# A decode layer on one core: the last 1,664 bytes a row of the modulation's weights loaded as 126 rows and 2 rows instead of 128

## Chip, cores, metric

One core of one Trainium2 chip. The metric is device time in microseconds (us) of one execution. Executions have a fast and a slow state (of the kernel before mostly 436.1 to 437.0 us, and 444.4 to 444.6). A ratio is the mean time of one kernel's fast runs over that of the other's fast runs of the same rounds, so it is not quite the ratio of the medians that are quoted.

## The reference, cut to what matters

```
mod = (silu(c) @ w_mod)                       # w_mod: 1024 x 6144, split into six shifts, scales and gates
h   = layernorm(x) * (1 + ca) + sa
x   = x + ga * attention(h, k_cache, v_cache, wq, wo)     # batch 8, 32 heads on 4 KV heads, 8192 keys of 128
h   = layernorm(x) * (1 + cb) + sb
x   = x + gb * ((relu(h @ W_gate) * (h @ W_up)) @ W_down) # 1024 -> 3584 -> 1024
```

All of it is bf16, one token for each of eight batches. The inputs are 185.6 MB, read once. That is what takes the time: 98.9% of sixteen DMA engines' span, by the page below.

## The kernel before

All weights and caches come through one ring in SBUF (`arena`, 128 partitions). SyncE issues the loads in a fixed order, each as soon as the part of the ring that it overwrites has been read.

```
def load(key, src, n, lo):
    place[key] = lo
    stream.append((key, src, n, lo))

def pump():
    while stream:
        key, src, n, lo = stream[0]
        if P.unread("arena", lo, lo + n):
            return
        stream.pop(0)
        dst = arena[:, lo:lo + n]
        P.op("sp", lambda e, dst=dst, src=src: e.dma_start(dst, src), writes=[slot_r(lo, lo + n)], dma=True, ...)
...
load(("wm", 0), wm_src[:, 0:D], D, 0)                    # D = 1024: the modulation's weights, 2,048 bytes a row,
load(("wm0", 0), wm_src[:, D:24 * D], 23 * D, D)         # 47,104 bytes a row,
load(("wm", 1), wm_src[:, 24 * D:48 * D], 24 * D, 24 * D) # 49,152 bytes a row
# [cut: wq in two loads; for each batch two K loads and a V load; wo, gate, up]
wd_parts = [(0, 14), (14, 21), (21, 25), (25, 27), (27, 28)]
for i, (r0, r1) in enumerate(wd_parts):
    load(("wd", i), d_src[:, r0 * D:r1 * D], (r1 - r0) * D, VPART + r0 * D)
```

The second half of the modulation's matmuls reads `slot_r(place["wm", 1], ... + 24 * D)`, so it waits for whatever loads fill that stretch.

Of the kernel before, what the change touches and what calls it, by code (L numbers as in the profile page):

```python
# [263 lines left out]
def bass_adaLN_cond__gqa_block_cached__glu_gated_reglu__decode_kernel(nc, A_x, A_k_cache, A_v_cache, A_wq, A_wo, B_x, B_W_gate, B_W_up, B_W_down, c, w_mod, out):  # L264
    B, _, D = A_x.shape
# [15 lines left out]
    KF = F // 128  # L281
    KO = Hq * Dh // 128
    FJ = F // 4

    P = Prog()
    holding = []
# [6 lines left out]
    with ExitStack() as es:  # L293
        E = es.enter_context

        def sb(name, shape, dtype):
            return E(nc.sbuf_tensor(name, shape, dtype))
# [4 lines left out]
        arena = sb("arena", [128, RING], dt.bfloat16)  # L302
# [38 lines left out]
        oX = ktb[:, 1024:2048].rearrange("p (k b) -> p k b", b=32)  # L341
        hrow = ktb[:, 2048:2048 + FJ]
        hmT = sb("hmT", [128, KF, 33], dt.bfloat16)
        xg = sb("xg", [64, 2, 256], dt.float32)
        rsel2 = sb("rsel2", [128, 64], dt.float32)
        grel = ktb[:, 4096:4096 + 2 * FJ].bitcast(dt.float32)
        r_oX, r_hmT = ("kt", 1024, 2048), ("hmT", 0, 1)
# [22 lines left out]
        def bank(b, n=1):  # L370
            return ("ps", b, b + n)

        def slot_r(lo, hi):
            return ("arena", lo, hi)
# [2 lines left out]

        stream, place = [], {}

        def load(key, src, n, lo):  # L380
            place[key] = lo
            stream.append((key, src, n, lo))

        def pump():
            while stream:
                key, src, n, lo = stream[0]
                if P.unread("arena", lo, lo + n):
                    return
                stream.pop(0)
                dst = arena[:, lo:lo + n]  # L390
                P.op("sp", lambda e, dst=dst, src=src: e.dma_start(dst, src), writes=[slot_r(lo, lo + n)], dma=True,  # L391
                     own=key[0] if key[0] in ("ka", "kb", "v") else None)
                if key[0] in ("ka", "kb", "v"):
                    P.held[key] = (lo, lo + n)

        wm_src = w_mod.rearrange("(p k) n -> p (k n)", k=KC)
# [3 lines left out]
        u_src = B_W_up.rearrange("(p k) n -> p (k n)", k=KC)  # L400
        d_src = B_W_down.rearrange("(p k) n -> p (k n)", k=KF)
        load(("wm", 0), wm_src[:, 0:D], D, 0)
        load(("wm0", 0), wm_src[:, D:24 * D], 23 * D, D)
        load(("wm", 1), wm_src[:, 24 * D:48 * D], 24 * D, 24 * D)
        wq_parts = [(0, 4), (4, 8)]
        for i, (r0, r1) in enumerate(wq_parts):
            load(("wq", i), wq_src[:, r0 * 4096:r1 * 4096], (r1 - r0) * 4096, 48 * D if i == 0 else 0)
# [11 lines left out]
        head = stream[2:]  # L419
        del stream[2:]  # L420
        pump()
        for t, src in enumerate((c.rearrange("b (j n) -> (b j) n", j=4), A_x.rearrange("b o (j n) -> (b o j) n", j=4))):
            P.op("act", lambda e, t=t, src=src: e.dma_start(cx[:, t, :], src), writes=[R("cx", t, t + 1)], dma=True)
        stream.extend(head)
        P.pump = pump
        pump()


# [102 lines left out]
        for i, (r0, r1) in enumerate(wq_parts):  # L531
            lo, hi = place["wq", i], place["wq", i] + (r1 - r0) * 4096
# [11 lines left out]
        for z in range(2):  # L544
            src = ps[:, 4 + z, :].rearrange("p (u x r) -> p u r x", u=J, r=2)
            dst = qs[:, 16 * z:16 * z + 16, :].rearrange("p (u r) x -> p u r x", r=2)
# [146 lines left out]
        for z in range(2):  # L693
# [6 lines left out]
            dst = orow[:, 4 * z:4 * z + 4, :].rearrange("p j d -> p (j d)")  # L700
# [34 lines left out]

        H = FJ // 2
        for nm, b0 in (("gate", 0), ("up", 2)):
            lo, hi = place[nm, 0], place[nm, 0] + KC * F
# [9 lines left out]
        for h in range(2):  # L748
            P.op("act", lambda e, h=h: e.activation(grel[:, H * h:H * h + H], ps[:, h, 0:H], ACT.Relu), reads=[bank(h)],
                 writes=[("kt", 4096 + FJ * h, 4096 + FJ * h + FJ)])  # L750
            P.op("dve", lambda e, h=h: e.tensor_tensor(out=hrow[:, H * h:H * h + H], in0=ps[:, 2 + h, 0:H],  # L751
                                                       in1=grel[:, H * h:H * h + H], op=ALU.mult),
                 reads=[bank(2 + h), ("kt", 4096 + FJ * h, 4096 + FJ * h + FJ)], writes=[("kt", 2048 + H * h, 2048 + H * h + H)])
        P.op("dve", lambda e: e.transpose(hmT[:, :, 1:33], hrow.rearrange("p (x k) -> p k x", k=KF)),  # L754
             reads=[("kt", 2048, 2048 + FJ), r_hmT], writes=[r_hmT])
        for i, (r0, r1) in enumerate(wd_parts):
            lo, hi = place["wd", i], place["wd", i] + (r1 - r0) * D
# [51 lines left out]
```

## Time and profile before

| kernel before | |
|---|---|
| median of the first three runs | 436.33 us (436.11 to 444.56) |
| profiled run | 444.49 us, slow state |
| bytes of the loads, share of sixteen DMA engines' span | 185.61 MB, 98.9% |
| end of the last load to end of the program | 3.0 us |

How to read it: the page counts sixteen DMA engines. A load of 128 rows leaves 128 packets in the trace, one a row, and sixteen landings, one an engine, so an engine has eight rows of such a load. The trace keeps the time of every landing. Sorted, they show how far apart the engines are, though not which is which. The lines of the profile are shown with the prediction, just below.

### The profile page before, as it was taken

What the parts mean: (1) busy time and instruction counts of PE and PEld (TensorE: products, weight loads), DVE (VectorE), ACT (ScalarE), POOL (GpSimd) and SP (SyncE); (2) the same over time, 40 slices, a digit from 0 to 9 for tenths busy, and PEclk for the clock granted to TensorE, in tenths of its full rate; (3) what the DMA queues carried; (4) which work ended last, traced back from release to release, by engine and by line L of the source; (5) the groups of instructions that cost most, each with busy time, mean ns of one, the idle gap of its engine ahead of it and who ended that gap; (6) DMA issues with size and microseconds to landing.
All of it is one profiled execution on the core that took longest, in us unless ns stands there. A gap on an engine that the chain in (4) does not pass through costs nothing. (4 is left out here: it accounts for less than half of the span.)

```text
span 443.1 us, 4774 instructions
## 1 busy us (share of the span) xinstructions
PE 263.3 (59%) x2139; PEld 138.0 (31%) x1979; DVE 249.0 (56%) x342; ACT 29.5 (7%) x54; POOL 8.7 (2%) x22
## 2 busy tenths in 40 slices
PE   0324336728865783886578388658838865365157
PEld 0100002218225421822542172154217215241015
DVE  0603028872985697298569729756972975421020
ACT  1100010020001002000100200010020010100000
POOL 3000000000000000000000000000000000000000
PEclk9976657978996997799599889959968996865668
DMA  9999999999999999999999999999999999999995
GB/s 367 417 355 390 404 385 426 379 417 430 467 396 420 456 444 420 429 470 390 435 476 408 423 429 467 420 423 473 399 420 426 467 455 402 452 416 419 439 414 239
DMA packets 5494, 185.74 MB, mean 419 GB/s; under 512 B 656, under 2 KB 752, under 8 KB 1136
## 3 DMA queue, kind: packets, MB, share of 16 engines
q1 hardware_dynamic: 5360, 185.61, 98.9%
q8 instruction: 5, 0.08, 0.1%
q10 hardware_dynamic: 128, 0.04, 0.0%
q14 instruction: 1, 0.01, 0.0%
HBM read 185.63 MB, written 0.02 MB: 419 GB/s over the span
## 5 line engine op out<-in xcount | busy, mean ns | idle before, releaser
L576 DVE STREAM_TRANSPOSE kt<-arena 128x1024 uint32<-128x1024 uint32 x128 | 148.2, 1211 | 64.4 <-DVEq L181 47.3
L586 PE MATMUL ps<-kt,qpad 128*128 128x512 bf16 x512 | 133.9, 384 | 44.1 <-DVE kt L576 38.1
L626 PE MATMUL ps<-arena,pT 128*64 128x256 bf16 x1024 | 74.5, 320 | 51.8 <-PEq L181 51.8
L626 PEld LDWEIGHTS ps<-arena,pT 128*64 128x64 bf16 x1024 | 72.0, 132 | 53.7 <-issue 53.1
L586 PEld LDWEIGHTS ps<-kt,qpad 128*128 128x128 bf16 x512 | 40.5, 98 | 133.7 <-DVE kt L576 101.0
L616 DVE TENSOR_SCALAR pT<-pd,mqf 128x1024 bf16<-128x1024 bf16 x64 | 28.2, 503 | 0.6
L608 ACT ACTIVATE prb<-ps,bias 128x1024 bf16<-128x1024 f32 x16 | 17.7, 1109 | 139.8 <-DVE mjt L603 139.8
L614 DVE STREAM_TRANSPOSE pd<-prb 128x1024 bf16<-128x1024 bf16 x16 | 19.8, 1239 | 10.9 <-ACT prb L608 10.9
L592 DVE TENSOR_REDUCE negm<-ps 128x1 f32<-128x512 f32 x32 | 21.2, 661 | 4.5 <-PE ps L586 4.5
L744 PE MATMUL ps<-arena,hT 128*32 128x448 bf16 x128 | 11.1, 535 | 16.8 <-DMA arena<-in_B_W_up_dram 11.4
L751 DVE TENSOR_TENSOR kt<-ps,kt 128x448 bf16<-128x448 f32 x2 | 1.2, 618 | 27.6 <-PE ps L744 27.6
L514 PE MATMUL ps<-arena,hT 128*32 128x512 bf16 x96 | 10.3, 615 | 9.7 <-DMA arena<-in_w_mod_dram 9.7
L538 PE MATMUL ps<-arena,hT 128*32 128x512 bf16 x64 | 7.2, 631 | 14.6 <-DMA arena<-in_A_wq_dram 14.6
L645 ACT ACTIVATE oacc<-ps 128x32 f32 (+1 forms) x9 | 1.8, 197 | 159.4 <-PE ps L640 159.4
L521 DVE COPY mod<-ps 128x512 f32<-128x512 f32 x2 | 1.3, 670 | 19.3 <-PE ps L514 19.3
L567 POOL TENSOR_TENSOR qpad<-qR,mq 128x128 bf16<-128x128 bf16 x8 | 4.9, 608 | 319.2 <-DVE pT L616 260.8
L549 DVE CAST kt<-ps 128x512 bf16<-128x512 f32 x1 | 0.7, 691 | 18.2 <-PE ps L538 18.2
L744 PEld LDWEIGHTS ps<-arena,hT 128*32 128x32 bf16 x64 | 2.4, 140 | 25.7 <-DMA arena<-in_B_W_up_dram 12.0
L763 PE MATMUL ps<-arena,hmT 128*32 128x256 bf16 x112 | 8.3, 309 | 3.5 <-DVE hmT L754 3.1
L714 PE MATMUL ps<-arena,kt 128*32 128x256 bf16 x128 | 5.9, 373 | 5.1 <-DMA arena<-in_A_wo_dram 5.1
L598 PE MATMUL ps<-identf,negm 128*128 128x128 f32 x16 | 3.9, 326 | 7.8 <-DVE negm L596 7.8
L763 PEld LDWEIGHTS ps<-arena,hmT 128*32 128x32 bf16 x112 | 6.5, 109 | 5.6 <-DMA arena<-in_B_W_down_dram 4.9
(87 smaller groups left out, 80.9 us busy)
## 6 DMA issues: line engine op xcount, KB each, us to landing
arena<-in_A_k_cache_dram SPq DMA_DIRECT2D x16, 4096.0 KB, 27.5
arena<-in_A_wq_dram SPq DMA_DIRECT2D x2, 4096.0 KB, 38.3
arena<-in_B_W_gate_dram SPq DMA_DIRECT2D x1, 7168.0 KB, 24.7
arena<-in_B_W_up_dram SPq DMA_DIRECT2D x1, 7168.0 KB, 27.9
arena<-in_w_mod_dram SPq DMA_DIRECT2D x1, 6144.0 KB, 33.4
arena<-in_w_mod_dram SPq DMA_DIRECT2D x1, 5888.0 KB, 17.8
arena<-in_B_W_down_dram SPq DMA_DIRECT2D x1, 3584.0 KB, 19.7
arena<-in_B_W_down_dram SPq DMA_DIRECT2D x1, 1792.0 KB, 23.6
```

Source lines behind the costliest of these rows:

```text
L514: fns.append(lambda e, w=w, pr=pr, j=j, kk=kk: hold(e.matmul(ps[32 * j:32 * j + 32, pr, :], hT[:, kk, :], w[:, 2 * pr:2 * pr + 2, j, :], s ...
L538: fns.append(lambda e, w=w, r=kk - r0, z=z, g=g, kk=kk: hold(e.matmul(ps[32 * g:32 * g + 32, 4 + z, :], hT[:, kk, :], w[:, r, g, z, :], st ...
L576: P.op("dve", lambda e_: e_.transpose(ktb[:, to:to + PART].bitcast(dt.uint32), arena[:, lo:lo + PART].bitcast(dt.uint32)), reads=[slot_r(l ...
L586: fns.append(lambda e_, t=t, r=r: e_.matmul(ps[:, e // 4, :].rearrange("p (c k) -> p c k", k=32), qpad[:, t * 2 + r, 24 - 8 * i:152 - 8 * ...
L592: P.op("dve", lambda e: e.tensor_reduce(negm[:, h:h + 1], ps[:, h, :], AX.X, ALU.max, negate=True), reads=[bank(h)] + (free(("ka", b)) if ...
L608: P.op("act", lambda e: e.activation(prb[:, f, :], ps[:, 2 * f:2 * f + 2, :].rearrange("p h n -> p (h n)"), ACT.Exp, bias=bias[:, 0:1], sc ...
L614: P.op("dve", lambda e: e.transpose(pd[:, f], prb[:, f]), reads=[R("prb", f, f + 1)], writes=[R("pd", 1024 * f, 1024 * f + 1024)])
L616: P.op("dve", lambda e, g=g: e.tensor_scalar(out=pT[:, f, :, :, g, :], in0=pd[:, f].rearrange("p (c i x) -> p c i x", c=32, i=2), scalar1= ...
L626: fns.append(lambda e, n=n, h=h, c_=c_, i=i, t=t: e.matmul(ps[64 * t:64 * t + 64, 5, 0:2 * Dh].rearrange("p (i d) -> p i d", d=Dh), pT[:, ...
L714: fns.append(lambda e, w=w, k=k, j=j: e.matmul(ps[32 * j:32 * j + 32, 5, 0:256], oX[:, k, :], w[:, k, j, :], start=(k == 0), stop=(k == KO ...
L744: fns.append(lambda e, w=w, kk=kk, h=h, j=j, b0=b0: hold(e.matmul(ps[32 * j:32 * j + 32, b0 + h, 0:H], hT[:, kk, :], w[:, kk, j, h, :], st ...
L763: fns.append(lambda e, w=w, r=k - r0, k=k, i2=i2, j=j: e.matmul(ps[32 * j:32 * j + 32, 4, 0:256], hmT[:, k, 1 - i2:33 - i2], w[:, r, i2, j ...
```

## The change

Two of the sixteen DMA engines are to carry 13 KB less, on the thought (an inference of the author's, not shown) that they are the ones that come last. The last 832 elements (1,664 bytes) a row of the modulation's weights are taken out of their load and brought by one of 126 rows and one of 2.

```
+    UNEVEN = [(832, 126)]
...
-        def load(key, src, n, lo):
+        def load(key, src, n, lo, dst=None):
             place[key] = lo
-            stream.append((key, src, n, lo))
+            stream.append((key, src, n, lo, arena[:, lo:lo + n] if dst is None else dst))
...
-        load(("wm", 1), wm_src[:, 24 * D:48 * D], 24 * D, 24 * D)
+        at1 = 48 * D - sum(n for n, rows in UNEVEN)
+        load(("wm", 1), wm_src[:, 24 * D:at1], at1 - 24 * D, 24 * D)
+        for n, rows in UNEVEN:
+            for lo, part in ((0, slice(0, rows)), (n // 2, slice(rows, 128))):
+                load(("wm1", n, lo), wm_src[part, at1:at1 + n], n // 2, at1 + lo, arena[part, at1:at1 + n])
+            at1 += n
```

More of the change, by code (lines that the diff above doesn't have):

```diff
@@ L378, in bass_adaLN_cond__gqa_block_cached__glu_gated_reglu__decode_kernel @@
         stream, place = [], {}
-        def load(key, src, n, lo):
+        def load(key, src, n, lo, dst=None):
             place[key] = lo
-            stream.append((key, src, n, lo))
+            stream.append((key, src, n, lo, arena[:, lo:lo + n] if dst is None else dst))
         def pump():
             while stream:
-                key, src, n, lo = stream[0]
+                key, src, n, lo, dst = stream[0]
                 if P.unread("arena", lo, lo + n):
@@ L389, in pump @@
                 stream.pop(0)
-                dst = arena[:, lo:lo + n]
                 P.op("sp", lambda e, dst=dst, src=src: e.dma_start(dst, src), writes=[slot_r(lo, lo + n)], dma=True,
```

## The prediction

It came to this: -0.49 us on the two spared engines, +0.14 us on the others (nine packets of 70 ns, 0.63 us, less 0.49), and +0.21 us on two of these that get a tenth packet. That 126 rows go to fourteen engines was assumed. That the two spared are the two last of the end (440.10 and 440.12) was the author's inference; "then they land at 440.11 - 0.49" starts from it, and the 0 in "-0.06 to 0 us" is the case in which the next laggard is one with a tenth packet (440.13). The forecast is 436.2 - 0.1 = 436.1 us.

> **What bounds the kernel now.** I read the page first: its row of DMA slices and its table of queues.
>
> ```profile
> DMA  9999999999999999999999999999999999999995
> ...
> q1 hardware_dynamic: 5360, 185.61, 98.9%
> q8 instruction: 5, 0.08, 0.1%
> ...
> q14 instruction: 1, 0.01, 0.0%
> ```
>
> The sixteen DMA engines are busy in every slice but the last. The loads (q1) take 98.9% of sixteen engines' span, for 185.61 MB. Two small queues fetch instructions on the same engines. No compute engine comes near: the page has PE at 59% and DVE at 56%. So the kernel streams its inputs once, and its time is the streaming time plus a head and a tail. Next, the sums by stretch (columns: stretch, length, busy time of PE, PEld, DVE, ACT, POOL, then granted clock, DMA share, GB/s):
>
> ```profile
> 5.00:45.00 40.00, 11.95 (x101) 2.29 (x37) 10.61 (x26) 2.50 (x4) 0.40 (x2) 0.84 1.00 389
> ...
> 120.00:160.00 40.00, 27.18 (x202) 14.54 (x202) 29.17 (x38) 2.50 (x5) 0.63 (x1) 0.91 1.00 433
> ```
>
> Both stretches have a DMA share of 1.00, but the first moves 389 GB/s and the other 433. The profiled run is one of the slow state (444.49 us). Its packets tell what that is: one of 32,768 bytes takes 1,353 to 1,361 ns for most of the first 80 us and 1,213 ns from there on. At the later rate those 80 us would have been about 80 x (1359 - 1213) / 1359 = 8.6 us shorter, and 444.5 - 8.6 = 435.9 is close to the two fast runs, 436.11 and 436.33. So I compare with 436.2, and read the tail of this profile as that of a fast run too.
>
> Then the chain of waits, its last pieces (start, duration, what):
>
> ```profile
> 413.18 26.30 DMA arena<-in_B_W_down_dram
> 439.49 0.04 issue
> 439.53 0.61 PE ps L763 x8
> 440.14 0.02 issue
> 440.16 0.41 PE ps L763 x4
> 440.58 0.02 issue
> 440.60 0.43 DVE lu L767
> 441.03 0.02 issue
> 441.05 0.42 DVE ob L769
> ```
>
> The end hangs on the last loads of W_down: eight matmuls, then four more, for the last two row groups, two vector instructions, the store. The last four matmuls start at 440.16, when the final load has landed on its slowest engine. Everything after that is fixed, 3.0 us to the span's end.
>
> Last, the issues in the timeline of SyncE:
>
> ```profile
> 0.00 1.44 SPq L391 DMA_DIRECT2D arena<-in_w_mod_dram  x3
> 1.57 23.59 SPq L391 DMA_DIRECT2D arena<-in_A_wq_dram  x2
> ...
> 343.66 0.33 SPq L391 DMA_DIRECT2D arena<-in_A_v_cache_dram  x1
> 361.64 0.33 SPq L391 DMA_DIRECT2D arena<-in_A_wo_dram  x1
> ```
>
> The load ahead of the V load issued at 343.66 is done on its first engine only at 348.66. That is the pattern of all batches: a load is issued at least some 5 us before any engine is through with the one ahead. So no engine runs dry, and a lag that one engine has picked up is neither lost nor made good: it is carried to the end.
>
> The trace keeps the sixteen completion increments of each load, one an engine, though not which engine gave which. The last load's are at 438.18 to 438.62 (ten engines), 439.10, and then 439.78, 439.82, 439.92, 440.10, 440.12. The program ends on the very last. Followed back, load by load, the six laggards left the pack one at a time, each after an instruction-fetch packet: 16,384 bytes at 50.17, 104.19, 393.79, 410.50 and 436.56 us (879 to 1,119 ns each), and 8,192 bytes at 84.72. A 16 KB fetch costs its engine about 1.2 to 1.6 us of lag, and each of the five fell on another engine.
>
> [...]
>
> **The change part by part.** Rates from the fast part of this trace: 32,768 bytes in 1,213 ns and 2,048 bytes in 84 ns, hence about 27.2 bytes a ns and 8 to 9 ns a packet. A packet of 1,664 bytes should take 61 + 9 = 70 ns (an estimate from those two).
> - Removed: the big load's rows shrink from 49,152 to 47,488 bytes. Each engine has eight of them, so 8 x 1,664 = 13,312 bytes less, 13,312 / 27.2 = 0.49 us on each of the sixteen.
> - Added: [...] Two more issues on SyncE, at 0.33 to 0.43 us each. They move the first wq issue from 1.57 to about 2.4 us, while the weights of the modulation land at 34.49: hidden by 30 us.
> - [...] Total bytes are unchanged, so the pack does not gain; only the two relieved engines move.
> - The matmuls on the second half of the weights must now wait for three loads instead of one. They start up to 0.2 us later at 34.5, with over 15 us of loads queued behind: not on the path that sets the end.
>
> What this does to the end depends on who is last. The engines of the two last increments at the end (440.10 and 440.12) come, followed back, from the late edge of the pack. One was hit by the first fetch: the first wq load's increments reappear in the second 10.75 us later, all but the one next to last, 45.25, which reappears at 57.64. The other was hit at 393.79, out of the pack's last two (387.79 and 387.81). [...] Then they land at 440.11 - 0.49 = 439.62, and the next laggard, 439.92, which got nine small packets, becomes the last: 439.92 + 0.14 = 440.06[...]. Against 440.12: -0.06 to 0 us. I choose -0.1 us, leaning a little to the gain because neighbouring small packets overlap: the last load has 8 x 2,048 bytes an engine and adds 0.62 to 0.65 us to the increments, where 8 x 84 would be 0.67.
>
> **Rivals.**
> - The two relieved engines alone set the end in unprofiled runs (the other fetches cost less there). For it: a fetch's cost differs with the traffic, 879 to 1,119 ns. Against it: three other engines are within 0.35 us of the last. It would give -0.49 us: 435.7.
> - The relieved engines are not among the laggards. For it: increments carry no engine. Then the last one gets its nine small packets for nothing, +0.14 to +0.21 us: 436.4.
> - The 126-row load is split over the engines in a way that makes them write across each other, or falls on far fewer engines. With one engine, it would take 126 x 70 = 8.8 us there, carried to the end: 445, slower by just 2%. The first would add some tenths. Nothing in this profile tells of it[...].
> - A wait replaces a wait: the two extra loads delay the modulation. Hidden, as worked out: no change.
>
> **Range and chances.** The centre is 436.2 - 0.1 = 436.1 us. The named outcomes lie between 435.7 and 436.4, and the two fast runs of before differ by 0.2 us; I add 0.3 to 0.5 us for runs on another chip: 435.4 to 436.9. A shift of 2% is 8.7 us, eighteen times the largest gain that 13 KB can give an engine, so "faster" gets 0.005. "Slower" gets 0.01, for the single-engine split or medians caught by the slow state; "within 2%" gets 0.985.
>
> **What would show it.** Right: the 126-row load's semaphore is at 2 at once and climbs by fourteen landings; among the last load's sixteen increments, two of the five latest move forward by about 0.6 us against the pack; the pack itself lands 0.1 to 0.2 us later; SyncE's first issues are five for the modulation; loads of wq, K and V keep their spacing (9.65 us for 4 MB). Wrong: increments of the last load in the old pattern[...], a pack later by more than 0.3 us (small rows dearer than 70 ns, or colliding), or a DMA share under 0.95 in a stretch that had 1.00 (an engine ran dry, and lags are not simply carried). A fast time under 435.4 would mean that the lags are worth more than this trace shows.

## The result

| | median us | range | runs |
|---|---|---|---|
| before | 436.7 | 436.11 to 444.56 | 6 |
| changed | 436.5 | 436.41 to 438.13 | 6 |

The ratio of the fast runs is 1.0003, 95% interval [0.9988, 1.0019]: the same. A second set on another chip (five runs against nine, told below) gave 1.001 [0.9996, 1.0024]. Nothing here is clear of noise in time. What the change did has to be read from the traces.

The changed kernel's profile is of the fast state. These lines answer to those in the prediction: first its DMA row, the same two queues, and two stretches of the sums by stretch (same columns).

```profile
DMA  9999999999999999999999999999999999999996
...
q1 hardware_dynamic: 5504, 185.61, 98.9%
q8 instruction: 5, 0.08, 0.1%
```

```profile
5.00:45.00 40.00, 13.97 (x133) 2.90 (x53) 10.60 (x26) 2.50 (x4) 0.40 (x2) 0.81 1.00 427
120.00:160.00 40.00, 28.37 (x203) 15.64 (x204) 29.02 (x38) 2.50 (x5) 0.63 (x1) 0.87 1.02 441
```

The loads move the same bytes in 144 more packets: 128 of 1,664 bytes and sixteen of 4 bytes, one for each new landing. The trace shows how the two small loads were shared out. The semaphore of the 126-row load has one update at 2.08 us, at its issue, and then fourteen landings, 31.53 to 32.26; that of the 2-row load one at 2.48 us and two landings, 31.99 and 32.08. That is nine rows and one, if they are shared out evenly. In the first stretch they move 427 GB/s where the slow profile of before had 389: that is the state, not the change. The kernel before in its fast state, run again as an experiment below, has 428 there, and its 32,768-byte packets take 1,213 ns from the start. (This view counts the whole of a packet in the stretch in which it starts. A share of 1.02 with 441 GB/s is thus no more than full, and in a short stretch one row of sixteen 32,768-byte packets, 0.52 MB, more or less moves the figure a good deal.)

Then SyncE's first issues in the timeline, and the end of the chain of waits, of the changed kernel:

```profile
0.00 2.31 SPq L391 DMA_DIRECT2D arena<-in_w_mod_dram  x5
2.35 22.06 SPq L391 DMA_DIRECT2D arena<-in_A_wq_dram  x2
```

```profile
403.30 20.43 DMA arena<-in_B_W_down_dram
423.73 0.04 issue
423.77 8.92 PE ps L768 x112
432.69 0.02 issue
432.71 0.43 DVE lu L772
433.14 0.02 issue
433.17 0.42 DVE ob L774
```

Five issues for the modulation instead of three, and the first wq issue at 2.35 us, as foreseen. The chain's end looks different from the slow profile: 112 matmuls in one piece after the first W_down load, with no wait for the last one. In fact two paths tie. The last load lands on its slowest engine at 432.23 us; its four matmuls (0.04 + 0.41 us, by the slow profile's chain) would end at 432.68, and the 112 end at 432.69. Both paths begin at the landing of the slowest engine, so the lag of the engines counts on either.

For a comparison within one state, the kernel before was run again (first experiment). Its chain ends like this:

```profile
402.91 20.35 DMA arena<-in_B_W_down_dram
423.26 0.04 issue
423.30 8.99 PE ps L763 x112
```

The landing that starts the matmuls is 0.47 us earlier there than in the changed kernel (423.26 against 423.73).

### The profile page after: what moved, and what is told of

Read it like the earlier page. It is cut to its first block, busy times and chain, and to the rows that moved or that the text cites. A ratio compares the mean times of both kernels' runs of the same rounds, so it can differ in the third digit from the quotient of the medians.

```text
span 435.2 us, 4777 instructions
## 1 busy us (share of the span) xinstructions
PE 260.5 (60%) x2139; PEld 137.9 (32%) x1979; DVE 249.1 (57%) x342; ACT 29.5 (7%) x54; POOL 8.8 (2%) x22
## 5 line engine op out<-in xcount | busy, mean ns | idle before, releaser
L749 PE MATMUL ps<-arena,hT 128*32 128x448 bf16 x128 | 9.8, 481 | 19.3 <-DMA arena<-in_B_W_up_dram 12.1
L543 PE MATMUL ps<-arena,hT 128*32 128x512 bf16 x64 | 7.2, 631 | 11.8 <-DMA arena<-in_A_wq_dram 11.8
L519 PE MATMUL ps<-arena,hT 128*32 128x512 bf16 x96 | 9.1, 559 | 8.3 <-DMA arena<-in_w_mod_dram 8.3
```

What stands on the lines that cost most here:

```text
L519: fns.append(lambda e, w=w, pr=pr, j=j, kk=kk: hold(e.matmul(ps[32 * j:32 * j + 32, pr, :], hT[:, kk, :], w[:, 2 * pr:2 * pr + 2, j, :], s ...
L543: fns.append(lambda e, w=w, r=kk - r0, z=z, g=g, kk=kk: hold(e.matmul(ps[32 * g:32 * g + 32, 4 + z, :], hT[:, kk, :], w[:, r, g, z, :], st ...
L749: fns.append(lambda e, w=w, kk=kk, h=h, j=j, b0=b0: hold(e.matmul(ps[32 * j:32 * j + 32, b0 + h, 0:H], hT[:, kk, :], w[:, kk, j, h, :], st ...
```

## The experiments

The landings and packet durations in this table are read from the traces. Head is the median landing of the second load, which no edit touches; all else is counted from it or from the last load, so that a slow start of a run (two have it, head at 17.9 us) drops out. The pack is the median of the ten earliest of the last load's sixteen landings.

| kernel | first wq packet on its 16 engines, ns, min / median / max | pack minus head, us | last landing minus pack, us | ratio to before [95%] |
|---|---|---|---|---|
| before, again | 1213 / 1213 / 1213 | 413.46 | 1.57 | 1.0005 [0.9988, 1.0022] |
| changed | 1471 / 1604 / 1616 | 414.02 | 1.44 | 1.0003 [0.9988, 1.0019] |
| changed, again | 1346 / 1552 / 1665 | 414.08 | 1.58 | 1.0010 [0.9996, 1.0024] |
| even split | 1213 / 1213 / 1214 | 413.58 | 2.07 | 1.0002 [0.9985, 1.0019] |
| 112 + 16 rows | 1325 / 1424 / 1440 | 413.68 | 1.92 | 1.0013 [0.9996, 1.0030] |
| even split, four times as wide | 1213 / 1213 / 1213 | 413.52 | 1.98 | see its text |
| 112 + 16, four times as wide | 1354 / 1882 / 2098 | 415.09 | 2.06 | 1.0032 [1.0016, 1.0049] |
| 126 + 2, four times as wide | 1359 / 1883 / 2367 | 415.33 | 1.71 | 1.0038 [1.0021, 1.0055] |

The theory that the prediction left me with (relief): the unequal load spares two engines half a microsecond (13,312 bytes at 27.2 bytes a ns), the rest pay only for their small packets. Its rival, raised when the changed kernel's trace showed the first wq packets at 1,471 to 1,616 ns: the packets of an uneven split and those of the loads beside it slow each other down (collision). The author thought it was because the rows change engines there; no trace has the engine of a row, so this cannot be shown. What the runs test is the slowing. In the changed kernel's trace the 1,664-byte packets start 66 ns apart on an engine, until engines that are already on wq appear; then packets take 75 to 118 ns instead of 69.

**The kernel before, again.** No edit.

> The kernel before, unchanged, for a profile in the fast state and for the noise of a ratio. All theories: ratio 1.000 within 0.002. In its profile the first packet of 32,768 bytes of the wq load takes 1,213 ns on each engine (in the changed kernel's profile it took 1,471 to 1,616 ns). The last load's sixteen landings have a pack of ten or so and six later ones, as in the slow profile; the two very last are 0.15 to 0.2 us behind the third last.

Measured: 436.42 us median (436.17 to 437.21), profile fast, first wq packets at 1,213 ns on all sixteen engines. The last load landed at 430.03 to 430.40 (ten engines), 431.09, 431.55, 431.71, 431.78, 431.78 and 431.80: a pack and six laggards. The three last are within 0.02 us, not 0.15 to 0.2 us apart from the third, so that detail of the slow profile was chance. Sparing two of the six can move the last landing by 0.02 us at most.

**Even split.** The same bytes in a load of their own, all 128 rows:

```
-            for lo, part in ((0, slice(0, rows)), (n // 2, slice(rows, 128))):
-                load(("wm1", n, lo), wm_src[part, at1:at1 + n], ...)
+            load(("wm1", n, rows), wm_src[:, at1:at1 + n], n, at1)
```

> The same last 1,664 bytes a row in a load of their own, but of all 128 rows, so that no engine is relieved: eight small packets on each. Relief theory (the small packets cost only their own time): every engine pays 8 x 66 ns less 0.49 us, 0.04 us later at the end, and the first wq packet takes 1,213 ns. Rival 1[...]: again 1,213 ns here[...]. Rival 2 (any load of small packets makes the first packets of the load behind it slow): 1,470 to 1,620 ns here too.

Measured: 436.66 us median (436.33 to 437.97), first wq packets at 1,213 ns, the pack 0.12 us later than before. So small packets as such do not stretch what follows; the second rival falls. The last landing was 2.07 us behind the pack: one engine that was already some 0.6 us behind the pack in the first wq load (42.82 against 42.24) was also hit by a fetch. That varies from run to run (1.44 to 2.07 in the table), so the last landing of a single profile is no measure to 0.3 us; the pack is.

**Four times as wide.** `UNEVEN = [(3328, 126)]`.

> The unequal load four times as wide: 6,656 bytes a row, 126 rows and 2. Relief theory: [...] Two landings move ahead of the pack by 2.3 us if these engines have no fetch, by 0.7 us or so where a fetch has thrown them back. The end is that of another laggard, +0.3 us: ratio 1.000 to 1.001. Collision theory: the stretch grows with the width of the rows, to 1.2 to 1.6 us for every engine in place of 0.26 to 0.40: the end +1.5 to +2 us, ratio 1.0035 to 1.0045.

Relief's sum: two engines have 53 KB less (-1.96 us), the others +0.32 us (9 x 0.253 less 1.96).

Measured: 438.06 us (437.99 to 438.28), ratio 1.0038: collision's figure, not relief's. The pack is 1.87 us later than before. It also tells engines apart. The first wq load landed at 41.17 and 41.20 on two engines and at 42.69 to 43.32 on the other fourteen: the two that were spared are 1.5 us ahead. After the fetch at 48.00 us the slot at 41.20 comes back 9.65 us later, at 50.85, as all do, and the slot at 41.17 is gone from the front. So one of the two spared engines carries that fetch. The other is first in every later load up to 430.31, against 431.90 for the next: it carries none.

**Stairs.** `UNEVEN = [(832, r) for r in (120, 126, 117, 108, 121, 100)]`, and more DMA semaphores.

> Six unequal loads of 1,664 bytes a row (120, 126, 117, 108, 121 and 100 rows, and what is left)[...]: by the packets' times +0.45, -0.38, -1.00, -1.62, -2.38 and -2.94 us[...]. It is to tell engines apart, not to be fast; its time is expected at 437 to 441 us. [...] A fetch then throws one named slot back by 1.2 to 1.6 us. [...] If none of them jumps, the change relieved engines that were not late.

The six figures are those of six engines that were to be relieved in steps, against +1.3 to +1.5 us on the other ten, and the two most relieved were to be the two that the changed kernel spares; "them" in the last sentence are their slots.

Measured: one run, 440.48 us. The front of the first wq load was 42.15, 42.23, 42.31, then 42.88, 43.49, 44.38 and the ten others from 45.05: six early slots, though the first three bunch, 0.16 us from first to third. The fetch at 49.07 threw back the slot at 42.23 (to 53.45, 1.56 us more than the rest). The fetches at 98, 390 and 403 us hit slots of the ten, and so did the one of 8,192 bytes at 80.90. So at least three of the five 16 KB fetches and four of all six fall on engines that these six loads did not bring to the front. That the two engines spared in the changed kernel are among the six at the front is assumed, not shown. The last fetch hit one of the six, which one stays open: the front engines had by then run into loads that were not yet issued, and their order was lost.

**120 rows and 8, four times as wide.** `UNEVEN = [(3328, 120)]`.

> 120 rows and 8 rows of 6,656 bytes: [...] One landing slot runs 1.2 to 2.2 us ahead of the pack in the wq loads. In the wider unequal load one of two leading slots was thrown back by the fetch at 48 us and the other never. [...] By the collision theory the first wq packets are stretched here too[...].

One engine alone was to be relieved, by 1.96 us, and its slot was to tell which of the two of the run with 126 rows carries the fetch.

Measured: one run, 439.30 us. One slot leads: 42.03 against 43.23 for the next in the first wq load, 51.68 after the fetch at 48.20, and still 431.19 against 432.46 at the end. It is never thrown back: the engine that is spared here has no fetch. Whether it is also the one of the two in the run with 126 rows that has none is not shown. First wq packets: 1,654 to 2,479 ns.

**112 rows and 16.** `UNEVEN = [(832, 112)]`: the loads' queue has 5,520 packets, the 5,360 of before, 128 small rows and 32 for landings, where 126 + 2 has 16. That is sixteen landings for each of the two loads, seven rows and one an engine if they are shared out evenly, so nobody is spared.

> The last 1,664 bytes a row as a load of 112 rows and one of 16: sixteen engines in both, seven rows and one, so that all engines carry the same bytes as before[...]. Collision theory[...]: the first wq packet is stretched from 1,213 to 1,450-1,620 ns although no engine is relieved, and the last small packets to 85-115 ns; the pack of the last load is 0.3 to 0.5 us later against the even split. Head-start theory (the stretch came from the two relieved engines being ahead): all first packets at 1,213 ns. In time either way 436.4 to 437.0, within the noise of a ratio.

Measured: 436.89 us (436.71 to 436.94), first wq packets at 1,325 to 1,440 ns, seven of the 128 small packets over 75 ns, the pack 0.10 us later than the even split's. The stretch is there with no engine ahead of another, so the head-start theory falls. It is half of what the 126-row load did, less than was expected.

**112 rows and 16, four times as wide.** `UNEVEN = [(3328, 112)]`.

> The same (112 rows and 16) with 6,656 bytes a row. Collision theory: the first packets of wq take 1.7 to 2.4 us as in the unequal load of this width, the end +1.0 to +1.6 us, ratio 1.0025 to 1.004. Head-start theory: ratio 1.000 and 1,213 ns.

Measured: 437.82 us (437.62 to 438.23), ratio 1.0032, first wq packets up to 2,098 ns, the pack 1.57 us later than that of its control below. This is the cleanest: the same bytes an engine and the same packet sizes; that the rows are dealt out as 112 and 16 is the only difference but one, a load more. The count of loads alone does not do it: it is the same at the narrow width, where the price was 0.10 us. The stretched packets make up the whole: against the control, the first wq packets have a mean of 0.65 us more on each engine and the 6,656-byte packets together 0.94 us; that is 1.59 us, where the pack is 1.57 us later.

**Even split, four times as wide** (the even split with 3,328 elements).

> The control for width: one load of 128 rows of 6,656 bytes, nothing crossed, nobody relieved. All theories that are still up: first wq packet 1,213 ns, ratio 1.000 within 0.0015. If it is 1.003 as the unequal one, the width or the number of loads is the cause and neither theory holds.

Measured: 436.67, 436.31, 436.19 and 440.94 us against a median of 436.36 for before. The ratio, 1.0034 [0.9978, 1.0089], is made by the one run at 440.94, which is counted as fast, and says nothing; the median is 436.49. The trace decides: 1,213 ns, 6,656-byte packets at 253 ns each (up to 595 in 112 + 16), the pack within 0.06 us of the kernel before.

The sums by stretch from 28 to 36 us show the direction of it from the outside, but not the size (columns as in the prediction; the last two are DMA share and GB/s). The kernel before, again:

```profile
28.00:36.00 8.00, 4.57 (x44) 0.60 (x16) 0.00 (x0) 0.00 (x0) 0.00 (x0) 0.50 0.99 426
```

The changed kernel:

```profile
28.00:36.00 8.00, 3.65 (x36) 0.68 (x16) 0.00 (x0) 0.00 (x0) 0.00 (x0) 0.50 0.96 388
```

The even split, four times as wide:

```profile
28.00:36.00 8.00, 4.04 (x40) 0.68 (x16) 0.00 (x0) 0.00 (x0) 0.00 (x0) 0.50 0.99 426
```

And 112 + 16 rows, four times as wide:

```profile
28.00:36.00 8.00, 2.18 (x24) 0.42 (x12) 0.00 (x0) 0.00 (x0) 0.00 (x0) 0.50 0.93 311
```

The changed kernel in its second profile (told just below):

```profile
28.00:36.00 8.00, 2.19 (x24) 0.42 (x12) 0.00 (x0) 0.00 (x0) 0.00 (x0) 0.50 1.02 411
```

The second line and the fifth are the same kernel, 388 and 411 GB/s: over 8 us, sixteen packets that start just inside or outside the stretch are worth 66 GB/s. With the bytes of each packet spread over its own time, the trace gives 433 GB/s for the kernel before, 409 and 407 for the changed one, 431 for the even split and 345 for 112 + 16, all with the engines busy for 1.00 to 1.01 of the stretch. The packets take longer, and a busy share alone would have hidden it.

**The changed kernel, again.** No edit of it.

> The changed kernel once more, in more rounds. Relief theory as predicted: -0.1 us, ratio 0.9998. Collision theory with the sizes of the runs so far (the pack of the last load 0.5 us later[...]): +0.2 to +0.4 us, ratio 1.0005 to 1.001. In the profile: first wq packets at 1,450 to 1,620 ns, one slot[...] ahead of the pack to the end by 0.1 to 0.4 us, the last landing of the last load at 432.1 to 432.5 us against 431.8 of the kernel before.

Collision's figures count one of the two spared engines as a laggard, and the other as the slot ahead, as the run four times as wide showed.

Measured: 436.75 us median (436.43 to 437.93) against 436.37, ratio 1.0010 [0.9996, 1.0024]; first wq packets 1,346 to 1,665 ns; the pack 0.62 us later than before; one slot ahead at the end, by 0.32 us. Its last landing was at 433.60, later than was expected, with a head 1.16 us later than that of the kernel before; less that, 432.44.

**More fetches.** The kernel before, with idle instructions on SyncE in four gaps in which it only waits:

```
+                if key[0] == "v" and 2 <= key[1] < 6:
+                    P.op("sp", [lambda e, i=i: e.sem_inc(spare, 1 - 2 * (i % 2)) for i in range(256)])
```

> The kernel before, with four times 256 idle semaphore instructions on SyncE, each batch in a gap in which SyncE only waits (before the V loads of four batches). No data moves differently. Theory (each instruction fetch of 16 KB costs the DMA engine that does it 1.2 to 1.6 us of loads, and the slowest engine's landing sets the end): four more packets of 16,384 bytes, one landing slot thrown back four times by 1.2 to 1.6 us, the end later by 3.3 to 6.5 us: ratio 1.008 to 1.015. Rival (a lag of one engine is absorbed in the slack of the queue): the slot is thrown back, the end moves by less than 0.5 us.

Measured: 440.20, 440.67, 445.65 us and one slow run, ratio 1.0156 [1.0098, 1.0214], slower but unclear by the 2% rule; the profiled run is the one at 440.20, 0.9% over the median of before in its rounds, and the others add scatter. Its queue and the end of its chain:

```profile
q14 instruction: 9, 0.07, 0.0%
```

```profile
427.26 0.04 issue
427.31 9.01 PE ps L766 x111
```

The fetches came as eight packets of 8,192 bytes on queue 14 (the kernel before has one there), not as four of 16,384. The last slot's distance to the pack grew from 1.8 us before the first of them to 5.3 us in the K load that landed at 268.77, 13 us after the eighth. From 221.81 us on, the V loads were issued 2.5 to 4.1 us later than before, since a load is read only when its slowest engine has landed, and then the other engines ran out of work too: at the end the pack is 2.3 us later and the last landing 4.06 us (435.86 against 431.80; 0.25 us of it was there before the first of these fetches). The idle instructions did not hold up the loads themselves: each batch of them ended 4.8 to 6.1 us before the V load that follows it was issued. So a fetch's lag is carried, and the slowest engine sets the end. The rival, slack that absorbs it, falls.

**The unequal load last of all.** The modulation in one load as before, and the last row group of W_down (2,048 bytes a row) as 126 rows and 2.

```
+            if i < 4:
                 load(("wd", i), d_src[:, r0 * D:r1 * D], (r1 - r0) * D, VPART + r0 * D)
+        for lo, part in ((0, slice(0, 126)), (D // 2, slice(126, 128))):
+            load(("wd4", lo), d_src[part, 27 * D:28 * D], D // 2, VPART + 27 * D + lo, arena[part, VPART + 27 * D:VPART + 28 * D])
+        place["wd", 4] = VPART + 27 * D
```

> The modulation's weights in one load as before; instead the last load of all, one row group of W_down (2,048 bytes a row), comes as 126 rows and 2. No 128-row load follows that it could meet. Collision theory[...]: only the load ahead and the small rows themselves can collide, for a few tenths; the pack of the last load, counted from the head of the run, at 413.5 to 413.8 us (kernel before 413.46, changed kernel 414.02 and 414.08)[...]. [...] +0.1 to +0.2 us, ratio 0.9995 to 1.001. [...]

Two engines were to be 0.6 us ahead by what they are spared, and the +0.1 to +0.2 us is for the end, set by a laggard of the other fourteen with one small packet more; relief alone was to give -0.2 to -0.4 us if the two spared were the last.

Measured: 436.82 us median (436.58 to 436.92) against 436.47; the ratio, 0.9986 [0.9916, 1.0057], is spoilt by a run of before at 441.17 and is inconclusive. The 126-row load landed at 430.43 to 430.83 on its first eight engines, around 413.9 us after the head, somewhat above what was expected, and at 432.25 on the last. Of the 128 packets of 4,096 bytes in the load ahead of it, 26 took more than 165 ns instead of 159; in the kernel before it was two (374 and 434 ns, beside the last fetch). So a price is paid with the load ahead as well; the last place does not save it.

No version here beats the kernel before, and none is recommended. In its fast profile the sixteen last landings have a mean of 430.75 us, and the last is at 431.80: no dealing-out of the same bytes could gain more than about 1.05 us, 0.24% (an estimate, with the fetches as they are), and in the stairs four of the six fetches hit engines that its six loads did not bring to the front.

## Why the prediction was right or wrong

The range and the class hold: a ratio of 1.0003, later 1.0010, where 436.1 against 436.2 was said; the gain of 0.1 us that was chosen is not clear of the noise either way. That the class held was no test, since 13 KB on an engine are worth 0.49 us, 0.1% of the time. And one of the prediction's own signs of being wrong came true: the pack of the last load was more than 0.3 us later. Two steps that made the sign of the change were wrong, and at four times the width they show: relief alone was expected to end at a ratio of 1.000 to 1.001, and 1.0038 was measured.

- **What bounds the kernel: right.** The slowest engine's last landing sets the end; in the fast profiles it is 2.98 to 3.05 us ahead of the end of the span (3.0 predicted), and 3.13 where the last load itself was split. What the slow profile hid is that the path through 112 matmuls ties with it.
- **The slow state: right.** The fast profile of before has 1,213 ns from the first 32,768-byte packet.
- **The +0.14 us on the engines that are not spared: wrong in size.** The pack was 0.56 and 0.62 us later. The packets' own part was right: 9 x 66 less 8 x 1,664 / 27.2 is 0.10 us, and the even splits cost 0.06 to 0.12. The missing term is the stretch: 0.26 to 0.40 us on the first wq packet of every engine, the spared ones included (mean 0.36), and 0.04 us an engine for dearer late small packets. With the 0.10 that makes 0.50 of the 0.56. The prediction had a guess of it among the rivals ("makes them write across each other", "some tenths") and gave it no weight because the trace of before could not show it.
- **The inference that the spared two are the two last: half right.** One of them carries the first fetch and is one of the laggards: in the run four times as wide its slot, at 41.17 us before the fetch at 48.00, is gone from the front after it. The other has none, and is first to the end (430.31 against 431.90); sparing it only made one slot early. For the start of the run the inference was good: an engine that has no small packet begins its first wq packet within 6 ns of the end of its part of the load ahead, and the two that do so ended that part 12th to 14th and last of the sixteen in each of the three traces with 126 rows (30.59 and 30.82 us, with the first engine at 30.22, in the changed kernel). But who is late at the end is settled by the fetches, and the one near 390 us, which the prediction gave to the other of the two, hit one of the ten slots behind in the stairs.
- **"Then they land at 440.11 - 0.49": wrong in the sum.** Of 0.49 us, the stretched packet takes back about 0.4: the first spared engine ended its packets of the first wq load at 40.67 us, where the sixteen ended at 40.38 to 40.77 in the kernel before.
- **The next laggard becomes the last: right in kind.** At least three 16 KB fetches fall on engines outside the six early ones of the stairs, and in the run four times as wide one of the two spared has no fetch at all.
- **A fetch costs 1.2 to 1.6 us and is carried: right.** It was 1.56 us in the stairs, and more fetches move the end.
- **The waits of the modulation: right that they are hidden, too small in size.** The second half of its matmuls starts at 32.34 us against 31.43, 0.9 us later and not 0.2, and the next K load is issued at 37.20 instead of 36.62, with wq loads queued until 50.8.

What stays open: how an uneven split stretches the packets. That rows of one load get in the way of another's is the author's conjecture, not shown: no trace here has the engine, the row or the place in memory of a packet. The runs show the cost of the split (the pack 1.57 us later for 6,656 bytes a row as 112 + 16), not whether it is the reading or the writing that is slowed. Nor is it settled by which sequencers the five 16 KB fetches were made, and why 126 + 2 stretched more than 112 + 16 at the narrow width.

## What to carry to other kernels

In a stream that fills all DMA engines with loads of 128 rows, try other row counts with care: those of 126, 120 and 112 rows stretched packets on all engines (the first of the next load 1,325 to 2,479 ns instead of 1,213), and a busy share of 1.00 does not show it, while the packets' durations do. Before sparing an engine, find out whether it is among the late ones: here a wide, deliberately unequal load put the two spared engines 1.5 us ahead, and one profile showed that one of them was thrown back and the other never. And find out how many: with six of sixteen late, sparing two hardly moves the end (by 0.02 us at most in the fast profile of before).
